# Turning the fourth row group of the first block by a transposing DMA in a fused S5 + SwiGLU kernel

## The chip, the cores and the metric

The kernel runs on one core of a Trainium2 chip. The metric is the device time of one execution in microseconds, lower is better. The core's engines are named as the profile names them: PE (TensorE, matrix products; PEld is its weight load), DVE (VectorE), ACT (ScalarE), POOL (GpSimd) and SP (SyncE, which here only issues DMAs).

## The reference

The input `x` has 2048 rows of 512 values. Its layer norm feeds two branches, and their sum with `x` is the output.

```python
def reference(x, Lambda_re, Lambda_im, B_re, B_im, C_re, C_im, log_dt, Dskip, w1, w3, w2):
    xn = layernorm(x)                                   # over the 512 values of a row
    Lam, dt = Lambda_re + 1j * Lambda_im, exp(log_dt)
    Lam_bar = exp(dt * Lam)
    B_bar = ((Lam_bar - 1) / Lam)[:, None] * (B_re + 1j * B_im)
    Bu = xn @ B_bar.T                                   # 2048 x 512, complex
    h[t] = Lam_bar * h[t - 1] + Bu[t]                   # recurrence over the rows
    ssm = 2 * (h @ (C_re + 1j * C_im).T).real + xn * Dskip
    glu = (silu(xn @ w1) * (xn @ w3)) @ w2              # 512 -> 1792 -> 512
    return x + ssm + glu
```

All tensors are bfloat16.

## The kernel before

The 2048 rows are cut into four blocks of 512 (`TBLK`), and a block into four row groups of 128. For the products over the 512 columns PE needs the normalised rows turned, columns on partitions: `xnT` holds a block as 4 x 128 columns by 512 rows. The 1792 features of `w1` and `w3` are cut into 14 groups of 128; the text calls such a group "a feature" and counts from 0.

The order of work on every engine is the program's order, written by hand (`manual_schedule`). It runs: the first block's layer norm and turning, `glu_up(0)` (products with w1 and w3, Silu and Copy on ACT, their product `hgT` on DVE), `ssm_in(0)` and `ssm_in(1)` (products with B), `glu_up(1)`, `y_out(0)` (products with w2 and C, output), and so on to `y_out(3)`. DVE's work of the recurrence, of the later blocks' layer norms (`ln_tasks`) and of the residual (`res_tasks`) is kept in a queue of tasks; `drain(rate)` in the loops above takes tasks from it by their assumed cost.

In blocks 1 to 3 the normalised rows are turned by transposing DMAs on SP (L232). In the first block PE turns them: `turn(c, ...)` issues four 128x128 transposes of row group `c` into a PSUM bank, `put(c, ...)` copies the result into `xnT`, on ACT for groups 0 and 1, on DVE for groups 2 and 3. Between these, `ahead(w_sbs, features, c, n)` issues the products of features 0 to 2 (`B3`) with row groups `c` to `c+n-1`, so that PE works on the groups that are there. The tiles of these three features, `begun`, hold six of the eight PSUM banks; `xt_a` and `xt_b`, the banks of the turned groups, hold the other two. `pprm`, the turned parameters of the recurrence, lies in `xt_a`; `par_cols` copies it on ACT. `glu_up(0)` then adds row group 3 to the features in `begun` (matmuls 128 wide) and makes the rest 512 wide; each feature's g and u tiles need a free PSUM bank.

SP's loads are issued in program order: two row groups of `x_blk[0]`, columns of features 0 to 3 of w1 and w3 in two parts each, of features 4 to 7, `x_blk[1]`, features 8 to 13, `dskip_row`, the turned B (`bt`, eight transposing DMAs), `x_blk[2]`. The parameters and the other two row groups of `x_blk[0]` come on ACT's queue. `load_rest` (w2, `x_blk[3]`, turned C) is a task of the queue.

Of the kernel before, what the change touches and what calls it, by code (L numbers as in the profile page):

```python
# [16 lines left out]
P = 128  # L17
# [3 lines left out]
def kernel(  # L21
# [24 lines left out]
    nc = tc.nc  # L46
# [8 lines left out]
    NDT = D // P  # L55
    NPT = PS // P
    NFT = F // P
# [3 lines left out]
    xv = A_x[0].rearrange("(b c p) d -> p b c d", p=P, c=CPB)  # L61
# [8 lines left out]
    def ps_tile(name):  # L70
        return psum.tile([P, 512], FP32, name=name, tag="ps")


    x_blk = [xpool.tile([P, CPB, D], BF16, name="x_blk") for _ in range(NBLK)]
# [7 lines left out]
    w1_sb = const.tile([P, NDT, F], BF16, name="w1_sb")  # L82
    w3_sb = const.tile([P, NDT, F], BF16, name="w3_sb")
    w2_sb = const.tile([P, NFT, D], BF16, name="w2_sb")
    w1v = B_w1.rearrange("(t p) f -> p t f", p=P)
    w3v = B_w3.rearrange("(t p) f -> p t f", p=P)

    H = NDT // 2

    def load_w13(f0, f1, parts=1):  # L90
        fs = slice(f0 * P, f1 * P)
        for w_sb, wv in ((w1_sb, w1v), (w3_sb, w3v)):
            for i in range(parts):
                ds = slice(i * NDT // parts, (i + 1) * NDT // parts)
                nc.sync.dma_start(out=w_sb[:, ds, fs], in_=wv[:, ds, fs])

    dskip_row = const.tile([P, D], BF16, name="dskip_row")
    bt = [const.tile([P, NDT, PS], BF16, name=f"bt{ri}") for ri in range(2)]
    ct = [const.tile([P, NPT, D], BF16, name=f"ct{ri}") for ri in range(2)]

    def load_turned(dst, src):
        for t in range(NDT):
            nc.sync.dma_start_transpose(out=dst[:, t, :], in_=src[:, t * P:(t + 1) * P])
# [9 lines left out]
    load_prm(1, A_Lambda_im, nc.scalar)  # L113
    load_prm(2, A_log_dt, nc.scalar)
    load_w13(0, 4, 2)
    load_w13(4, 8)
    nc.sync.dma_start(out=x_blk[1], in_=xv[:, 1, :, :])
    load_w13(8, NFT)
    nc.sync.dma_start(out=dskip_row, in_=A_Dskip.partition_broadcast(P))
    load_turned(bt[0], A_B_re)  # L120
    load_turned(bt[1], A_B_im)
    nc.sync.dma_start(out=x_blk[2], in_=xv[:, 2, :, :])

    def load_rest():
        nc.sync.dma_start(out=w2_sb, in_=B_w2.rearrange("(t p) d -> p t d", p=P))
# [19 lines left out]
    begun = [(ps_tile("g_ps"), ps_tile("u_ps")) for _ in range(3)]  # L145
# [13 lines left out]
    xnTs = [None] * NBLK  # L159
# [28 lines left out]
    def normed(c, parts=1):  # L188
        xn = work.tile([P, D], BF16, name="xn", bufs=8)
        for i in range(parts):  # L190
            ds = slice(i * D // parts, (i + 1) * D // parts)
            nc.vector.tensor_scalar(out=xn[:, ds], in0=x_blk[c // CPB][:, c % CPB, ds], scalar1=mv_all[:, c, 0:1],
                                    scalar2=rstd_all[:, c:c + 1], op0=ALU.subtract, op1=ALU.mult)
        return xn
# [49 lines left out]
    xt_a = psum.tile([P, 2 * NDT, P], BF16, name="xt_ps", tag="ps")  # L244
    xt_b = psum.tile([P, 2 * NDT, P], BF16, name="xt_ps", tag="ps")
    pprm = xt_a[:, NDT]
    xn0 = xns_of[0] = {}

    def turn(c, pxt, d0=0, d1=NDT):
        for dt in range(d0, d1):  # L250
            nc.tensor.transpose(out=pxt[:, dt - d0, :], in_=xn0[c][:, dt * P:(dt + 1) * P], identity=ident)  # L251

    def put(c, pxt, eng, d0=0, d1=NDT):
        dst = xnTs[0][:, d0:d1, c * P:(c + 1) * P]
        if eng is nc.scalar:
            nc.scalar.activation(out=dst, in_=pxt, func=ACT.Copy)
        else:
            nc.vector.tensor_copy(out=dst, in_=pxt)
# [10 lines left out]
    def par_cols():  # L269
        prmc = const.tile([P, 3 * NPT], FP32, name="prmc")  # L270
        nc.scalar.activation(out=prmc, in_=pprm[:, :3 * NPT], func=ACT.Copy)
        col["lre"], col["lim"], col["ldt"] = (prmc[:, i * NPT:(i + 1) * NPT] for i in range(3))
        nc.scalar.activation(out=c4("dt"), in_=col["ldt"], func=ACT.Exp)
        nc.gpsimd.tensor_tensor(out=c4("kr"), in0=col["dt"], in1=col["lre"], op=ALU.mult)
        nc.gpsimd.tensor_tensor(out=c4("ki"), in0=col["dt"], in1=col["lim"], op=ALU.mult)
        nc.gpsimd.tensor_scalar(out=c4("turn"), in0=col["ki"], scalar1=float(1.0 / (2.0 * np.pi)), scalar2=None,
                                op0=ALU.mult)
        tt = nc.gpsimd.tensor_tensor
        tt(out=c4("den"), in0=col["lre"], in1=col["lre"], op=ALU.mult)
        tt(out=c4("d2"), in0=col["lim"], in1=col["lim"], op=ALU.mult)  # L280
        tt(out=col["den"], in0=col["den"], in1=col["d2"], op=ALU.add)
# [87 lines left out]
    def glu_mm(b, f, w_sb, ps, ts, dts=range(NDT), joins=False):  # L369

        for dt in dts:
            nc.tensor.matmul(out=ps[:, ts], lhsT=w_sb[:, dt, f * P:(f + 1) * P], rhs=xnTs[b][:, dt, ts],  # L372
                             start=(dt == 0 and not joins), stop=(dt == NDT - 1))
# [128 lines left out]
    def ahead(w_sbs, fs, c, n=1, dts=range(NDT), joins=False):  # L502
        for f in fs:
            for w_sb in w_sbs:
                glu_mm(0, f, w_sb, begun[f][w_sb is w3_sb], slice(c * P, (c + n) * P), dts, joins)

    t1 = [ps[:, :P].bitcast(BF16).rearrange("p (t c) -> p t c", c=P) for ps in begun[2]]
    ta, tb, t2, t3 = xt_a[:, :H], xt_b[:, :H], xt_b[:, NDT:], xt_a[:, :NDT]

    stats(0)  # L510
    aggr(0)
# [19 lines left out]
    B3 = (0, 1, 2)  # L531
    lo, hi = range(H), range(H, NDT)
# [5 lines left out]
    rstd_act(3, 4)  # L538
    ahead((w3_sb,), B3, 0, 2, lo)
    turn(2, t2)  # L540
    put(2, t2, nc.vector)
    xn0[3] = normed(3)
    ahead((w3_sb,), B3, 0, 2, hi)
    nc.tensor.transpose(out=pprm, in_=prm, identity=ident)  # L544
    par_cols()
    ahead((w1_sb, w3_sb), (0,), 2)
    turn(3, t3)
    put(3, t3, nc.vector)
    nc.scalar.activation(out=r_col, in_=col["kr"], func=ACT.Exp)
    nc.scalar.preload_act_table_set("silu_and_others")  # L550
    ahead((w1_sb, w3_sb), (1, 2), 2)

    push([(3.2, par_turns), (0.2, par_recip)])
    push([(0.0, lambda: for_act.extend(par_trig()))])
# [53 lines left out]
```

## Time and profile before

| what | value |
|---|---|
| median of 3 runs | 211.85 us (211.66 to 211.96) |
| profiled execution | 212.11 us |
| its span, first to last instruction | 210.3 us |
| granted TensorE clock | 1.00 throughout |
| PE busy | 206.6 us (98%) |
| DVE busy | 173.5 us (82%) |
| ACT busy | 93.4 us (44%) |
| DMA bytes | 13.69 MB, mean 65 GB/s |

The share of busy time is an average over the span; the chain that ended last says which engine's work followed on which without a gap. A timeline row gives start, duration, engine, line, operation and tiles. Matmuls overlap in PE's pipeline, so the cost of a matmul is the distance to the next start, not its duration. "SPq" rows are the issue of DMAs; "to landing" is from the start of the issue to the signal that the data are there.

### The profile page before, as it was taken

What the parts mean: (1) busy time and instruction counts of PE and PEld (TensorE: products, weight loads), DVE (VectorE), ACT (ScalarE), POOL (GpSimd) and SP (SyncE); (2) the same over time, 40 slices, a digit from 0 to 9 for tenths busy, and PEclk for the clock granted to TensorE, in tenths of its full rate; (3) what the DMA queues carried; (4) which work ended last, traced back from release to release, by engine and by line L of the source; (5) the groups of instructions that cost most, each with busy time, mean ns of one, the idle gap of its engine ahead of it and who ended that gap; (6) DMA issues with size and microseconds to landing.
All of it is one profiled execution on the core that took longest, in us unless ns stands there. A gap on an engine that the chain in (4) does not pass through costs nothing.

```text
span 210.3 us, 2878 instructions
## 1 busy us (share of the span) xinstructions
PE 206.6 (98%) x1036; PEld 97.7 (46%) x1036; DVE 173.5 (82%) x346; ACT 93.4 (44%) x167; POOL 6.0 (3%) x27
## 2 busy tenths in 40 slices
PE   8999999999999999999999999999999999999994
PEld 3864444444444444444444444444444444444453
DVE  4699989989999999999999999999999999121111
ACT  3599967666666200066666600036666620000000
POOL 2010320000000000000000000000000000000000
PEclk9999999999999999999999999999999999999999
DMA  5999599944000000000004200100000000000110
GB/s 165 294 366 219 109 178 325 217 106 100 0 3 0 0 25 25 28 26 0 0 0 77 28 1 24 50 25 5 0 0 0 0 3 25 27 25 25 34 44 25
DMA packets 25014, 13.69 MB, mean 65 GB/s; under 512 B 15912, under 2 KB 25000, under 8 KB 25000
## 3 DMA queue, kind: packets, MB, share of 16 engines
q1 hardware_dynamic: 24704, 13.24, 26.1%
q10 hardware_dynamic: 296, 0.27, 0.4%
q8 instruction: 8, 0.13, 0.3%
q14 instruction: 6, 0.05, 0.1%
HBM read 7.74 MB, written 2.10 MB: 47 GB/s over the span
## 4 chain that ended last, share of the span: by engine, by line
PE 96%; DMA 2%; SPq 0%; DVE 0%; issue 0%
PE g_ps L372 23%; PE u_ps L372 23%; PE y_ps L488 23%; PE y_ps L493 13%; PE bu_ps L411 13%; DMA w_sb<-in_B_w_dram 2%; SPq L77 0%; PE xt_ps L251 0%; DVE o L498 0%; PE xt_ps L544 0%
## 5 line engine op out<-in xcount | busy, mean ns | idle before, releaser
L372 PEld LDWEIGHTS <-w_sb 128*128 128x128 bf16 x502 | 46.4, 98 | 50.6 <-DMA w_sb<-in_B_w_dram 0.6
L372 PE MATMUL g_ps<-xnT,w_sb 128*128 128x512 bf16 (+2 forms) x254 | 58.2, 354 | 0.3 <-DMA w_sb<-in_B_w_dram 0.3
L372 PE MATMUL u_ps<-xnT,w_sb 128*128 128x512 bf16 (+2 forms) x248 | 58.4, 358 | 0.0
L488 PE MATMUL y_ps<-w_sb,hgT 128*128 128x512 bf16 (+2 forms) x238 | 51.2, 366 | 0.0
L390 ACT ACTIVATE up<-u_ps 128x512 bf16<-128x512 f32 x56 | 34.0, 607 | 14.9 <-PE u_ps L372 14.9
L413 ACT ACTIVATE u<-bu_ps 128x512 bf16<-128x512 f32 x32 | 19.1, 597 | 46.3 <-PE bu_ps L411 46.3
L388 ACT ACTIVATE sl<-g_ps 128x512 bf16<-128x512 f32 x56 | 34.0, 608 | 9.9 <-PE g_ps L372 9.2
L445 DVE TENSOR_TENSOR_SCAN ab<-r_col,h,ab 128x256 bf16<-128x256 f32 x56 | 37.7, 733 | 0.2
L488 PEld LDWEIGHTS <-hgT 128*128 128x128 bf16 x238 | 22.8, 98 | 25.9
L498 DVE TENSOR_TENSOR o<-y_ps,x_blk 128x512 bf16<-128x512 f32 (+2 forms) x17 | 11.1, 654 | 24.3 <-PE y_ps L493 24.3
L493 PE MATMUL y_ps<-ct,h 128*128 128x512 bf16 (+2 forms) x136 | 30.4, 366 | 0.0
L411 PE MATMUL bu_ps<-xnT,bt 128*128 128x512 bf16 x128 | 28.1, 379 | 0.0
L397 DVE TENSOR_TENSOR hgT<-sl,up 128x512 bf16<-128x512 bf16 x56 | 22.9, 414 | 2.1 <-ACT up L390 2.1
L493 PEld LDWEIGHTS <-h 128*128 128x128 bf16 x136 | 13.0, 98 | 14.7
L411 PEld LDWEIGHTS <-bt 128*128 128x128 bf16 x128 | 12.5, 98 | 15.1
L164 DVE BATCH_NORM_STATS2 stats<-x_blk 128x6 f32<-128x512 bf16 x16 | 10.6, 675 | 2.5 <-DMA x_blk<-in_A_x_dram 2.5
L454 DVE TENSOR_TENSOR ab<-ab,tab_s 128x2048 bf16<-128x2048 bf16 x8 | 9.8, 1222 | 0.2
L450 DVE TENSOR_TENSOR ab<-ab,tab_c 128x2048 bf16<-128x2048 bf16 x8 | 9.8, 1222 | 0.1
L427 DVE TENSOR_TENSOR ab<-u,tab_x 128x2048 bf16<-128x2048 bf16 x8 | 9.7, 1219 | 0.0
L430 DVE TENSOR_TENSOR ab<-u,tab_y 128x2048 bf16<-128x2048 bf16 x8 | 9.7, 1218 | 0.0
L201 DVE TENSOR_TENSOR x_blk<-xd,x_blk 128x512 bf16<-128x512 bf16 x16 | 6.8, 426 | 0.5
L200 DVE TENSOR_TENSOR xd<-xn,dskip_row 128x512 bf16<-128x512 bf16 x16 | 6.7, 418 | 0.0
(76 smaller groups left out, 81.3 us busy)
## 6 DMA issues: line engine op xcount, KB each, us to landing
out_dram<-o SPq DMA_DIRECT2D x15, 128.0 KB, 1.7
w_sb<-in_B_w_dram SPq DMA_DIRECT2D x1, 1792.0 KB, 9.3
x_blk<-in_A_x_dram SPq DMA_DIRECT2D x3, 512.0 KB, 6.3
w_sb<-in_B_w_dram SPq DMA_DIRECT2D x2, 768.0 KB, 7.8
w_sb<-in_B_w_dram SPq DMA_DIRECT2D x4, 256.0 KB, 5.0
w_sb<-in_B_w_dram SPq DMA_DIRECT2D x2, 512.0 KB, 4.1
x_blk<-in_A_x_dram SPq DMA_DIRECT2D x2, 128.0 KB, 2.2
x_blk<-in_A_x_dram ACTq DMA_DIRECT2D x1, 256.0 KB, 4.7
```

The lines of the kernel that those rows point to most:

```text
L164: nc.vector.bn_stats(out=sums[c], in_=x_blk[c // CPB][:, c % CPB, :])
L372: nc.tensor.matmul(out=ps[:, ts], lhsT=w_sb[:, dt, f * P:(f + 1) * P], rhs=xnTs[b][:, dt, ts], start=(dt == 0 and not joins), stop=(dt == ...
L388: nc.scalar.activation(out=sl16, in_=g_ps, func=ACT.Silu)
L390: nc.scalar.activation(out=up16, in_=u_ps, func=ACT.Copy)
L397: nc.vector.tensor_tensor(out=hg[b][:, f, :], in0=sl16, in1=up16, op=ALU.mult)
L411: nc.tensor.matmul(out=u_ps, lhsT=bt[ri][:, dt, pt * P:(pt + 1) * P], rhs=xnTs[b][:, dt, :], start=(dt == 0), stop=(dt == NDT - 1))
L413: nc.scalar.activation(out=u16[:, :, pt, ri, :], in_=u_ps.rearrange("p (s t) -> p s t", s=NSB), func=ACT.Copy)
L445: nc.vector.tensor_tensor_scan(out=a[:, pt, 2 * ri + 1, :], data0=r_b, data1=a[:, pt, 2 * ri, :], initial=init, op0=ALU.mult, op1=ALU.add)
L450: nc.vector.tensor_tensor(out=a[:, :, 0::2, :], in0=a[:, :, 1::2, :], in1=tab_b("c"), op=ALU.mult)
L488: nc.tensor.matmul(out=y_ps[:, ds], lhsT=hg[b][:, f, cl * P:(cl + 1) * P], rhs=w2_sb[:, f, ds], start=(f == 0), stop=False)
L493: nc.tensor.matmul(out=y_ps[:, ds], lhsT=h_tiles[i][:, pt, ri, h_ts], rhs=ct[ri][:, pt, ds], start=False, stop=(pt == NPT - 1 and ri == 1))
L498: nc.vector.tensor_tensor(out=o16[:, ds], in0=y_ps[:, ds], in1=x_blk[b][:, cl, ds], op=ALU.add)
```

## The change

- The fourth row group (c = 3) of the first block is turned by one transposing DMA on SP, from its normalised rows straight into `xnT`. The four transposes on PE and the copy on DVE go; the tile view `t3` goes.
- The SP loads from w3 of features 4 to 7 on are put into a function `load_next`, called right behind that DMA. The w1 load of features 4 to 7 stays ahead of it.
- On DVE the normalising of group 3 now comes before `put` of group 2.
- On PE the transpose of `prm`, and with it `par_cols`, moves ahead of the second half of w3's products with groups 0 and 1.
- A fourth pair of PSUM tiles is added to `begun`: the products of feature 3 are issued with the others, first w1 on groups 0 and 1, then group 2 of features 0 to 2, then w3 on groups 0 and 1 and both weights on group 2. `glu_up(0)` finishes four features with row group 3, not three.

```diff
     load_w13(0, 4, 2)
-    load_w13(4, 8)
-    nc.sync.dma_start(out=x_blk[1], in_=xv[:, 1, :, :])
-    load_w13(8, NFT)
-    nc.sync.dma_start(out=dskip_row, in_=A_Dskip.partition_broadcast(P))
-    load_turned(bt[0], A_B_re)
-    load_turned(bt[1], A_B_im)
-    nc.sync.dma_start(out=x_blk[2], in_=xv[:, 2, :, :])
+    nc.sync.dma_start(out=w1_sb[:, :, 4 * P:8 * P], in_=w1v[:, :, 4 * P:8 * P])
+
+    def load_next():
+        nc.sync.dma_start(out=w3_sb[:, :, 4 * P:8 * P], in_=w3v[:, :, 4 * P:8 * P])
+        nc.sync.dma_start(out=x_blk[1], in_=xv[:, 1, :, :])
+        load_w13(8, NFT)
+        nc.sync.dma_start(out=dskip_row, in_=A_Dskip.partition_broadcast(P))
+        load_turned(bt[0], A_B_re)
+        load_turned(bt[1], A_B_im)
+        nc.sync.dma_start(out=x_blk[2], in_=xv[:, 2, :, :])
...
-    ta, tb, t2, t3 = xt_a[:, :H], xt_b[:, :H], xt_b[:, NDT:], xt_a[:, :NDT]
+    ta, tb, t2 = xt_a[:, :H], xt_b[:, :H], xt_b[:, NDT:]
...
     ahead((w3_sb,), B3, 0, 2, lo)
     turn(2, t2)
+    xn0[3] = normed(3)
     put(2, t2, nc.vector)
-    xn0[3] = normed(3)
-    ahead((w3_sb,), B3, 0, 2, hi)
+    nc.sync.dma_start_transpose(out=xnTs[0][:, :, 3 * P:], in_=xn0[3])
+    load_next()
     nc.tensor.transpose(out=pprm, in_=prm, identity=ident)
     par_cols()
-    ahead((w1_sb, w3_sb), (0,), 2)
-    turn(3, t3)
-    put(3, t3, nc.vector)
+    ahead((w3_sb,), B3, 0, 2, hi)
+    begun.append((ps_tile("g_ps"), ps_tile("u_ps")))
+    ahead((w1_sb,), (3,), 0, 2)
+    ahead((w1_sb, w3_sb), B3, 2)
+    ahead((w3_sb,), (3,), 0, 2)
+    ahead((w1_sb, w3_sb), (3,), 2)
     nc.scalar.activation(out=r_col, in_=col["kr"], func=ACT.Exp)
     nc.scalar.preload_act_table_set("silu_and_others")
-    ahead((w1_sb, w3_sb), (1, 2), 2)
```

## The prediction

> **What bounds the kernel now.** I read the page's busy rows and its chain that ended last, PE's waits, then the timeline of the first 30 us, then single DMA issues with their times to landing.
>
> ```profile
> span 210.3 us, 2878 instructions
> PE 206.6 (98%) x1036; PEld 97.7 (46%) x1036; DVE 173.5 (82%) x346; ACT 93.4 (44%) x167; POOL 6.0 (3%) x27
> ...
> PE 96%; DMA 2%; SPq 0%; DVE 0%; issue 0%
> ```
> ```profile
> PE g_ps L150 <- PEq L592: 0.8, 1, 0.8
> PE g_ps L372 <- DMA w_sb<-in_B_w_dram: 0.3, 1, 0.3
> ```
>
> PE is busy 98% of the span and holds 96% of the chain. The second fence is all that PE waited for: 0.8 us at the start, and 0.3 for the first weights, which end at 6.48 us (the chain's 2% DMA). From there to the end PE never waits. So the time moves by exactly two things: PE work added or removed, and PE waits added. The timeline around the change (start, duration, engine):
>
> ```profile
> 8.46 0.20 ACT L172 ACTIVATE rstd_all<-rstd_all 128x1 f32<-128x1 f32 x1
> 8.49 0.39 PE L251 MATMUL xt_ps<-ident,xn 128*128 128x128 bf16 x4
> ...
> 8.72 0.82 PE L372 MATMUL u_ps<-xnT,w_sb 128*128 128x256 bf16 x6
> 8.92 0.42 DVE L258 COPY xnT<-xt_ps 128x512 bf16<-128x512 bf16 x1 [0.73 <-PE xt_ps L251]
> 9.26 0.40 DVE L192 TENSOR_SCALAR xn<-x_blk,mv_all,rstd_all 128x512 bf16<-128x512 bf16 x1
> ...
> 9.37 0.22 PE L544 MATMUL xt_ps<-ident,prm 128*128 128x128 bf16 x1
> ...
> 9.88 0.39 PE L251 MATMUL xt_ps<-ident,xn 128*128 128x128 bf16 x4
> ...
> 10.10 0.39 PE L372 MATMUL g_ps<-xnT,w_sb 128*128 128x128 bf16 x4
> ...
> 12.33 1.03 PE L372 MATMUL g_ps<-xnT,w_sb 128*128 128x512 bf16 x4
> ...
> 13.20 1.03 PE L372 MATMUL u_ps<-xnT,w_sb 128*128 128x512 bf16 x4
> ```
>
> Durations overlap in PE's pipeline, so costs are differences of starts: four transposes 9.88 to 10.10, 0.22; four 128-wide matmuls 0.2225 (10.10 to 10.99 is four such sets); six 256-wide 8.72 to 9.37, 0.65, so 0.433 for four; four 512-wide 12.33 to 13.20, 0.864; the turn of `prm` 0.06.
>
> Two DMA prices follow, from the rows of single issues: the transposing DMA at 111.17 (ring empty) and the 512 KB load of `w1_sb` columns 4 to 8 (issued 6.45).
>
> ```profile
> L232 SPq DMA_TRANSPOSE xnT<-xn x1: 1201/1201/1201, 111.2 to 111.2; - x1
> ...
> DMA to landing us min/median/max: 2.3/2.3/2.3
> ```
> ```profile
> w_sb<-in_B_w_dram SPq DMA_DIRECT2D x1, 512.0 KB, 4.1
> ```
>
> A transposition holds SP 1.2 us and lands 2.3 us after its issue began.
>
> **Part 1, PE work.** Removed: four transposes, 0.22. Feature 3 (index from 0) of columns 0 to 511 is done as 256+128+128 in place of 512: per weight 0.433+0.2225+0.2225 = 0.878 for 0.864, twice, +0.03. Laid out from the last unchanged start, 8.72: `prm` to 8.78, the w3 half of features 0 to 2 to 9.43, feature 3 w1 to 9.86, six sets of group 2 (1.335) to 11.20, feature 3 w3 to 11.63, its two sets of group 2 to 12.08. There `glu_up` needs group 3 for the first time (10.99 before). Eight sets of group 3 end at 13.86, where feature 4 starts; before it was 14.06. So **-0.20** if PE never waits. DVE's `put` of group 3 (0.42) goes too, off the path.
>
> **Part 2, the new wait for the transposition.** DVE has group 3's rstd at 8.66 and normalises at once, 8.72 to 9.13, since `put` of group 2 now stands behind it. SP starts 0.16 after such an end (the row at 110.60 lasts 0.41, SP starts at 111.17), so at 9.29, and the data land at 9.29+2.3 = 11.6. PE wants them at 12.08: hidden by 0.5, cost 0 taken. The cover is the fourth feature and group 2, 2.65 us of matmuls from 9.43. Ends: 2.3 (ring empty) and 4.7 (the transposition at 24.94, directly behind a 512 KB load), which would land at 13.99 and cost 1.9. I take the near end, because the load ahead on this ring was issued 2.84 us before, not 0.7, and should land near 6.45+4.1 = 10.55.
>
> The VectorE page of the Trainium skill ("VectorE: DVE Perf Modes", section The three transpose paths) speaks against the change: it gives a 128x128 block 390 ns on TensorE and 1309 ns on the DMA crossbar, and advises TensorE. By its figure four blocks in a row would be 5.24 us (an estimate), landing at 14.53, and the sum 2.45-0.20, some 2.2 us slower; the rows here, 2.3 to 4.7 for the same four blocks, replace it.
>
> **Part 3, PSUM.** The fourth pair of tiles needs both banks of `xt_a` and `xt_b`. One is free after the copy of `pprm` on ACT (about 9.2), the other after DVE's `put` of group 2, now 9.17 to 9.59. If the w1 tile takes the second, PE waits from 9.43 to 9.65: 0 to 0.22. The trace doesn't show which; I take 0, and part 4 would swallow most of it.
>
> **Part 4, the loads moved behind it on SP.** Behind the waiting SP stand, in order, w3 columns 4 to 8, `x_blk[1]`, w1 and w3 from 8, `dskip_row`, eight turned loads of B, `x_blk[2]`. The first was issued at 6.86 and is now at 9.29+1.22+0.04 = 10.55. PE wants it for feature 4's up half at 13.86+0.86 = 14.72. With 4.1 it lands at 14.65, just in time. But a load that follows transpositions moves data later: `x_blk[2]`, issued 24.23 right behind such DMAs, against w1's of 6.45 (window, us, clock, DMA share, GB/s):
>
> ```profile
> 7.20:7.40 0.20, 1.00 0.16 46
> 7.40:7.60 0.20, 1.00 0.89 97
> ...
> 25.20:25.60 0.40, 1.00 0.06 18
> 25.60:26.00 0.40, 1.00 0.34 108
> ```
>
> Data start 0.95 after the issue there, 1.4 here, so 4.5 in place of 4.1 (an estimate): landing 15.05, a wait of **+0.33**, the value taken. Ends: 4.1 (no wait) and 6.3, the row of `x_blk[1]`, 512 KB among other loads (landing 16.85, a wait of 2.13).
>
> The others are covered. `x_blk[1]` lands about 1.4 behind, 16.4 (13.7 before); DVE's statistics, at 14.64 now, stall some 1.8, and `hgT` of feature 2 behind them goes to about 17.0, while ACT wants its `sl16` buffer for feature 6 at 19.27; DVE waits 1.26 at 47.75, so its lag ends there. Were that cover gone, PE would wait out the rest, at most 1.8. w1 from 8 landed at 15.8, is some 2.8 later, 18.6, and is wanted at 20.8. The last turned load of B goes from 22.9 to about 26, lands 2.7 later at 28.7, wanted at 32.3. The transpositions of block 1 land about 34, wanted at 38.4. ACT's first Silu moves from 11.88 to 12.5; feature 4's PSUM bank is then free at 13.1, wanted at 13.86. Cost 0.
>
> **Sum.** -0.20+0.33 = +0.13 against the profiled execution's 212.11 (span 210.3), which lies 0.26 above the median 211.85. So 211.98, put as 212.0. About 0.2% (0.42 us) is what this measurement can tell from no change.
>
> **Rivals.** (a) *The transposition queues.* The load of w1 columns 4 to 8 is still in flight at 9.29. If the transposition meets it as at 24.94 and 26.3 (4.7 and 4.1), it lands at 13.4 to 14.0, PE waits 1.3 to 1.9, and the time is 213.0 to 213.6. It decides from 3.4 us to landing (12.7). For it: those two rows. Against it: 2.84 us of head start. The DMA page of the Trainium skill ("DMA: Bandwidth & Descriptors", section Queues, rings and completion order) says that an engine consumes a ring's descriptors in order; the rows at 24.94 agree. Chance 0.14.
>
> (b) *The w3 load lands late*, at 5.0 to 6.3 after issue, as the first 256 KB loads (4.8 to 5.2) and `x_blk[1]` (6.3) did in company. PE waits 0.83 to 2.13 at feature 4: +0.63 to +1.93, 212.5 to 213.8. It is slower by over 0.42 from 4.8 on. For it: it is the first load issued again after 2.6 us, with 2 MB issued right behind it. Against it: so was w1's at 6.45, with 4.1. Chance 0.20.
>
> (c) *Faster.* With no wait at all 211.65, which is inside the 0.2%. For more, a wait of before would have to go: past the start PE's only one is the 0.3 for the first weights, whose issues stand unchanged ahead of the edit. Without it the time would be 211.35. Chance 0.06.
>
> **Numbers.** Forecast 0.60 (211.6 to 212.3: the w3 load landing 4.1 to 4.8 after its issue), (a) 0.14, (b) 0.20, (c) 0.06. Faster 0.06, same 0.60, slower 0.34. The range 211.5 to 213.2 takes in the forecast, the lower part of (a) and most of (b).
>
> **What would show it.** After: twelve transposes on PE, not sixteen; one more transposing DMA near 9.3 landing near 11.6; group 3's first matmul at 12.1 without idle time before it; feature 4's up half at 15.05 with some 0.3 idle, released by the w3 load; its gate half at 13.86. Idle time before group 3 means (a), over 0.8 before feature 4's up half means (b), 0.2 before feature 3 means the PSUM bank. Wrong in kind would be a wait after 25 us, say for B or for `x_blk[2]`, which I price at nothing.

## The result, and the profile after

The changed kernel takes 212.41 us (median of 10 runs, 212.05 to 212.60) against 211.81 (211.62 to 211.96) for the kernel before: a ratio of 1.0028, 95% interval 1.0018 to 1.0037. It is slower by 0.6 us. The profiled execution took 212.46 us, 0.35 more than that of before. From the page of the profile after:

```profile
PE 206.3 (98%) x1048; PEld 97.9 (46%) x1048; DVE 173.3 (82%) x345; ACT 93.2 (44%) x167; POOL 6.6 (3%) x27
...
PE 91%; DMA 4%; DVE 1%; ACT 1%; SPq 0%; issue 0%
```

PE's share of the chain fell from 96 to 91%; DMA's rose from 2 to 4%, and DVE and ACT have 1% each. PE's waits (us in total, times, longest) name two more than before, the second and the fourth:

```profile
PE g_ps L153 <- PEq L598: 0.8, 1, 0.8
PE u_ps L375 <- DMA w_sb<-in_B_w_dram: 0.4, 1, 0.4
PE g_ps L375 <- DMA w_sb<-in_B_w_dram: 0.3, 1, 0.3
PE xt_ps L254 <- DVE xn L195: 0.2, 1, 0.2
```

The fourth is at 4.91, ahead of the first weights, for which PE waits anyway. The timeline shows where the second is:

```profile
8.60 0.41 DVE L195 TENSOR_SCALAR xn<-x_blk,mv_all,rstd_all 128x512 bf16<-128x512 bf16 x1 [0.51 <-ACT rstd_all L175]
...
9.03 1.30 SPq L546 DMA_TRANSPOSE xnT<-xn  x1
...
10.39 0.57 SPq L119 DMA_DIRECT2D w_sb<-in_B_w_dram  x1
...
11.76 0.39 PE L375 MATMUL u_ps<-xnT,w_sb 128*128 128x128 bf16 x4
11.98 0.39 PE L375 MATMUL g_ps<-xnT,w_sb 128*128 128x128 bf16 x4
...
13.77 1.03 PE L375 MATMUL g_ps<-xnT,w_sb 128*128 128x512 bf16 x4
...
15.17 1.04 PE L375 MATMUL u_ps<-xnT,w_sb 128*128 128x512 bf16 x4 [0.38 <-DMA w_sb<-in_B_w_dram]
...
16.60 0.69 DVE L167 BATCH_NORM_STATS2 stats<-x_blk 128x6 f32<-128x512 bf16 x1 [1.58 <-DMA x_blk<-in_A_x_dram]
```

SP starts the transposition 0.02 us after DVE's normalised rows. PE passes to row group 3 at 11.98 without a gap, 0.22 after the set before it. Feature 4's up half comes 1.40 us after its gate half, 0.864 without a wait, so 0.54 is lost to the w3 load issued at 10.39. (The 0.38 in brackets is less, since ends of matmuls are modelled.) The chain that ended last shows what that load hangs on:

```profile
1.53 4.62 DMA x_blk<-in_A_x_dram
...
8.60 0.41 DVE xn L195
9.01 0.34 DVE xnT L261
9.35 0.99 SPq L546
...
10.39 4.74 DMA w_sb<-in_B_w_dram
...
15.17 1.04 PE u_ps L375 x4
```

(It puts SP's release down to DVE's copy that ends at 9.34, though the issue had begun at 9.03, when the rows of L195 were there.) Before, the chain ran through the first weights and then PE alone. Now it runs from the last rows of `x_blk[0]` through the layer norm on DVE and ACT to SP, the load, and PE.

### The profile page after: what moved, and what is told of

The parts are those of the page before. It is cut to its first block, busy times and chain, and to the rows that moved or that the text cites. A ratio compares the mean times of both kernels' runs of the same rounds, so it can differ in the third digit from the quotient of the medians.

```text
span 210.7 us, 2902 instructions
## 1 busy us (share of the span) xinstructions
PE 206.3 (98%) x1048; PEld 97.9 (46%) x1048; DVE 173.3 (82%) x345; ACT 93.2 (44%) x167; POOL 6.6 (3%) x27
## 4 chain that ended last, share of the span: by engine, by line
PE 91%; DMA 4%; DVE 1%; ACT 1%; SPq 0%; issue 0%
PE y_ps L491 23%; PE u_ps L375 21%; PE g_ps L375 21%; PE y_ps L496 13%; PE bu_ps L414 13%; DMA w_sb<-in_B_w_dram 2%; DMA x_blk<-in_A_x_dram 2%; SPq L546 0%; DVE xn L195 0%; ACT L81 0%; DVE stats L167 0%; ACT rstd_all L175 0%; ACT rstd_all L174 0%; DVE xnT L261 0%; DVE mv_all L170 0%
## 5 line engine op out<-in xcount | busy, mean ns | idle before, releaser
L375 PEld LDWEIGHTS <-w_sb 128*128 128x128 bf16 x518 | 47.1, 98 | 50.4 <-DMA w_sb<-in_B_w_dram 1.4
L195 DVE TENSOR_SCALAR xn<-x_blk,mv_all,rstd_all 128x512 bf16<-128x512 bf16 (+1 forms) x18 | 6.3, 392 | 0.6 <-ACT rstd_all L175 0.5
```

## The experiments

Two theories at first. L (the late load): PE's work is 0.2 us less, the wait for w3 of features 4 to 7 eats that and more, and nothing else happened. R (a rest elsewhere): part of the 0.60 us has another source, because the pair of profiles shows 0.35 only. Diffs are against the changed kernel unless said.

**same_again.** No edit.

> The changed kernel itself, unaltered, on the same chip as the next ones. Both theories: about 212.4 us (before 211.8), with feature 4's up half starting 1.4 us after its gate half instead of 0.86, because the w3 load of features 4 to 7 lands at about 15.1. Theory L (the late load): the wait of about 0.54 us, less 0.2 us of PE work saved, is all there is, and the median lies 0.35 to 0.6 above before according to when that load lands in a run. Theory R (a rest elsewhere): the profile explains only 0.35 of the 0.60 us between the medians, and 0.25 us come from something that the trace of PE doesn't show.

Measured: 212.18 us against 211.79, ratio 1.0017 (1.0007 to 1.0027). In its profile SP issued the transposition at 8.85, and the up half followed 0.96 us after the gate half:

```profile
13.76 1.03 PE L375 MATMUL g_ps<-xnT,w_sb 128*128 128x512 bf16 x3
14.72 1.04 PE L375 MATMUL u_ps<-xnT,w_sb 128*128 128x512 bf16 x4
```

The wait is 0.10 here, 0.54 in the first profile: its size differs between executions, and the total with it (212.00 and 212.46). The w3 load was issued 0.19 earlier here (10.20, not 10.39), as the last rows of `x_blk[0]` came earlier, and it took 4.47 us to land, not 4.74; PE's own marks up to there are the same to 0.01.

**halves_4_6.**

```diff
-    nc.sync.dma_start(out=w1_sb[:, :, 4 * P:8 * P], in_=w1v[:, :, 4 * P:8 * P])
+    load_w13(4, 6)
     def load_next():
-        nc.sync.dma_start(out=w3_sb[:, :, 4 * P:8 * P], in_=w3v[:, :, 4 * P:8 * P])
+        load_w13(6, 8)
```

> The same bytes ahead of the transposing DMA as in the change, but w1 and w3 of features 4 and 5 (256 KB each) instead of w1 of features 4 to 7 (512 KB); behind it both weights of features 6 and 7. PE wants the loads behind the transposition at 17.2 us instead of 14.6, and they should land by about 15.5. Theory L: no wait of PE past 6.5 us but the first weights' own, and the time is 0.2 below before: 211.6 us. Theory R: the wait goes, 0.54 us, but the rest stays: 211.85 us, the same as before.

Measured: 211.88 against 211.79, ratio 1.0011 (0.9997 to 1.0026). Three of its twelve runs lie at 212.44 to 213.11, the other nine at 211.67 to 212.08.

```profile
13.50 1.03 PE L375 MATMUL g_ps<-xnT,w_sb 128*128 128x512 bf16 x3
14.36 1.03 PE L375 MATMUL u_ps<-xnT,w_sb 128*128 128x512 bf16 x4
```

The wait is gone in this trace, yet the median is R's (211.85), not L's (211.6): a rest exists, though not on PE, which in this trace is 0.18 us ahead of before from w3's first products (7.46) on.

**w3_ahead.**

```diff
-    nc.sync.dma_start(out=w1_sb[:, :, 4 * P:8 * P], in_=w1v[:, :, 4 * P:8 * P])
+    load_w13(4, 8)
     def load_next():
-        nc.sync.dma_start(out=w3_sb[:, :, 4 * P:8 * P], in_=w3v[:, :, 4 * P:8 * P])
```

> The w3 load of features 4 to 7 is issued ahead of the transposing DMA again, so that 1 MB stands in front of it on SP's ring and not 512 KB. Theory Q (the transposition has to queue behind the loads of its ring): the load's data end at about 11.2 us and the transposition lands some 1.9 us later, near 13.0; PE, which wants row group 3 at 12.0, waits about 1 us, and no longer for w3: 212.6 us. Rival (a transposition takes 2.3 us whatever is on the ring): it lands at 11.4, nothing waits, 211.6 us.

Measured: 212.05 against 211.79, ratio 1.0019 (1.0000 to 1.0039). SP issued the transposition at 8.82; PE got to row group 3 at 12.20, 0.21 late:

```profile
11.76 0.39 PE L374 MATMUL u_ps<-xnT,w_sb 128*128 128x128 bf16 x4
12.20 0.38 PE L374 MATMUL g_ps<-xnT,w_sb 128*128 128x128 bf16 x4
```

With 1 MB ahead on the ring it is slower, 3.3 us from issue to landing and 3.4 to PE's start, but by less than I expected (4.0, from 9.03 to 13.0). Its first packets move 1.9 us after its issue, at 10.73, when the last of the loads ahead go; in the profile after they move 1.3 us after the issue, at 10.32, when the 512 KB ahead have been gone since 9.8. The DMA page of the Trainium skill ("DMA: Bandwidth & Descriptors", section Queues, rings and completion order) has descriptors of a ring consumed in order on each engine; the order of the packets in this trace agrees.

**three_features.**

```diff
-    begun.append((ps_tile("g_ps"), ps_tile("u_ps")))
-    ahead((w1_sb,), (3,), 0, 2)
     ahead((w1_sb, w3_sb), B3, 2)
-    ahead((w3_sb,), (3,), 0, 2)
-    ahead((w1_sb, w3_sb), (3,), 2)
```

> The change without the fourth feature: group 3 is still turned by DMA and the loads are still behind it, but PE has only group 2 of three features to do in the meantime (1.3 us from 9.3 on). This shows when the transposition lands, which the change hides. Theory: it lands 2.3 to 2.4 us after its issue at 9.03, so at 11.4; PE wants it at 10.65, waits 0.75 us, and reaches feature 4's up half at about 15.2, when w3 is there. The time is about 0.35 to 0.45 above before, 212.2 us. Rival (the transposition is slowed by the w1 load in flight, 3 us or more): a wait of 1.4 us or more and 212.8 us or more.

Measured: 212.41 against 211.79, ratio 1.0025 (1.0014 to 1.0036).

```profile
10.15 0.39 PE L375 MATMUL u_ps<-xnT,w_sb 128*128 128x128 bf16 x4
11.02 0.38 PE L375 MATMUL g_ps<-xnT,w_sb 128*128 128x128 bf16 x4 [0.48 <-DMA xnT<-xn]
```

Issued at 8.51, used at 11.02: 2.5 us with 512 KB ahead, where 2.3 was predicted for the change. PE loses 0.65 (0.87 less 0.222) rather than 0.75, as PE gets there later after the issue than I had reckoned; the median is 0.2 above what was expected. So the fourth feature does what it is there for: it hides this wait, which the change without it pays.

**early_turn.**

```diff
-    nc.sync.dma_start_transpose(out=xnTs[0][:, :, 3 * P:], in_=xn0[3])
+    nc.sync.dma_start_transpose(out=xnTs[0][:, :, 3 * P:], in_=xn0[1])
```

> The changed kernel with one operand altered: the transposing DMA reads the normalised rows of group 1, ready at 5.3 us, not those of group 3 (so the products of row group 3 are computed from group 1's rows). SP then doesn't wait for DVE, the loads behind go out some 2 us earlier, and neither the transposition nor the w3 load can be late. What is left is the change in PE's work alone. Theory L: 0.2 us below before, 211.6 us, and from the start of w3's first products to the last matmul 199.0 us in the trace (199.22 before, 199.59 after). Theory R: something else in the change costs 0.2 to 0.25 us, and the time is that of before, 211.8, or above.

Measured: 211.65 against 211.77, ratio 0.9994 (0.9985 to 1.0002). From 7.76 to the last group of matmuls at 206.79 it is 199.03 us, as theory L had it, and no wait is left behind the first weights. The medians lie 0.12 us apart, less than the 0.2, and the interval takes in no difference at all; -0.18 of PE work and +0.09 at the end (both read below) would make -0.09. PE's work and the number of DMAs are those of the change, and only the time at which the transposition and the loads behind it go out differs. So the late issue is what costs the change its 0.60 and 0.39: against their own runs of before it lies 0.72 and 0.51 above early_turn.

**x_before_w3.**

```diff
-        nc.sync.dma_start(out=w3_sb[:, :, 4 * P:8 * P], in_=w3v[:, :, 4 * P:8 * P])
         nc.sync.dma_start(out=x_blk[1], in_=xv[:, 1, :, :])
+        nc.sync.dma_start(out=w3_sb[:, :, 4 * P:8 * P], in_=w3v[:, :, 4 * P:8 * P])
```

> The changed kernel with the first two loads behind the transposition swapped: 512 KB of x_blk[1] go ahead of w3 of features 4 to 7. The suspected wait is made longer by a known amount: w3 is issued 0.6 us later and lands behind 512 KB at 370 GB/s, 1.4 us later, at about 16.5. Theory L (PE waits for this load and nothing hides it): the wait grows by 1.4 to 2 us and so does the time, to 213.6 to 214.3. Rival (the load's wait is mostly hidden by other slack): less than half of that, under 213.1.

Measured: 213.41 against 211.77, ratio 1.0078 (1.0065 to 1.0091).

```profile
13.28 1.03 PE L375 MATMUL g_ps<-xnT,w_sb 128*128 128x512 bf16 x4
16.00 1.04 PE L375 MATMUL u_ps<-xnT,w_sb 128*128 128x512 bf16 x4 [1.69 <-DMA w_sb<-in_B_w_dram]
```

The wait is 2.72-0.864 = 1.86 us, and the total is 1.64 above before: 1.86-0.18 = 1.68. The wait goes into the time whole, to some 0.1 us, with no slack to hide it. From the transposition's issue (8.36) to the up half it is 7.64 us, against 6.14 and 5.87 in the two profiles of the change: 1.5 to 1.8 more, as expected. The median is 0.2 below L's range all the same: it lies 1.0 and 1.2 above the two medians of the change, to which the growth was added, while the profiled waits grew by 1.3 and 1.8. Waits in the unprofiled runs of the change that are longer than the profiled ones would explain that, and early_turn's medians point the same way.

**act_ring.** The transposing DMA on ACT's queue, the loads up to `dskip_row` where they were before.

```diff
-    nc.sync.dma_start_transpose(out=xnTs[0][:, :, 3 * P:], in_=xn0[3])
-    load_next()
     nc.tensor.transpose(out=pprm, in_=prm, identity=ident)
     par_cols()
+    nc.scalar.dma_start_transpose(out=xnTs[0][:, :, 3 * P:], in_=xn0[3])
+    load_next()                    # only bt and x_blk[2]
```

> The loads are issued on SP as in the kernel before, none waits for DVE, and the transposing DMA is issued on ACT's queue, behind the copy and the exponential of par_cols (about 9.1 us). Only x_blk[2] and the turned B stay behind it. It tells whether the transposition is late because of its place in SP's ring or because all transfers share the engines. Theory S (shared engines, in w3_ahead it took 3.4 us from issue to PE's start with 1 MB ahead on its own ring): 3 us or more here too, landing at 12.1 or later, PE waits 0.2 to 1 us before row group 3, 211.8 to 212.6 us. Rival (a ring of its own brings it past the loads): it lands within 2.5 us, nothing waits, and the time is 211.6.

Measured: 220.12 against 211.77, ratio 1.0401 (1.0378 to 1.0424). The issue at 9.01 took 9.5 us to land; the first fence is PE's wait, the second the windows (us, granted clock, DMA share, GB/s):

```profile
PE g_ps L374 <- DMA xnT<-xn: 6.6, 1, 6.6
```
```profile
15.00:16.00 1.00, 1.00 0.06 9
16.00:17.00 1.00, 0.74 1.08 338
17.00:18.00 1.00, 0.50 1.10 382
```

A ring of its own does not bring it past the 3 MB of loads issued on SP by then: its own packets move from 13.3 to 17.7, side by side with those of the last loads, with next to nothing moving from 15 to 16 us, and it lands at 18.5. The direction was S's, the size far off. With the loads held back, on SP's ring, it took 2.5 us; the run changes the ring and the loads at once, so how much of the 7 us is due to each is not shown, nor why the traffic stopped for a microsecond. PE's idle time also halved the granted clock from 17 to 23 us: the eight sets of row group 3 took 3.37 us, not 1.78, and feature 4's gate half 1.54, not 0.86, another 2.3. With the 6.7 of the wait (11.63 to 18.58, less 0.22) that is the 9.0 by which the profiled execution (220.76) lies above before. The page "TensorE: Matmul & The Clock Gate" of the Trainium skill (Part 1, on the clock gate) has the clock fall to half after an idle window of some 3.4 us; here it is 0.74 in the stretch that begins 4 us after PE's last matmul (12.0).

**before_again.** The kernel before, no edit.

> The kernel before once more, for a second profile: the first one has its first matmul on real data at 6.48 us and its total 0.3 us above the median of the unprofiled runs. If the arrival of the first weights varies between executions, the first matmul is at another time here and the total moves with it, while the time from the first products of w3 to the last matmul stays 199.2 us.

Measured: 211.66 us.

Every mark from w3's first products on (7.40, 13.62, 14.48) is 0.43 or 0.44 earlier than in the first profile of before, and the total is 0.45 less. The first products with loaded weights start at 5.92, not 6.48: PE does not wait for the weights here, while it waited 0.31 us there. Two profiles of one kernel differ by more than the change's profiled loss. The rows of `x_blk[0]` come earlier too: the statistics of group 2 start at 5.66, not 6.27. Side by side (us; "end" is from the start of the last DVE instruction to the execution's end; DMAs are all issues on SP and ACT):

| run | w3's first products | feature 4, gate | feature 4, up | end | total | DMAs |
|---|---|---|---|---|---|---|
| before | 7.83 | 14.06 | 14.92 | 4.41 | 212.11 | 64 |
| before_again | 7.40 | 13.62 | 14.48 | 4.40 | 211.66 | 64 |
| after | 7.72 | 13.77 | 15.17 | 4.50 | 212.46 | 65 |
| same_again | 7.72 | 13.76 | 14.72 | 4.49 | 212.00 | 65 |
| early_turn | 7.76 | 13.80 | 14.66 | 4.49 | 211.93 | 65 |
| halves_4_6 | 7.46 | 13.50 | 14.36 | 4.64 | 211.78 | 67 |

The distance from w3's first products to feature 4 is 6.22 or 6.23 before, 6.04 or 6.05 in every form of the change without an earlier wait: 0.18 saved. The last columns hold a part of the rest: the end is 0.09 longer in the change, 0.24 in halves_4_6. In halves_4_6 that is nearly all: -0.18+0.24 = 0.06, for 0.09 between the medians.

**w2_in_four** and **sevens** followed. The first is the kernel before with

```diff
-        nc.sync.dma_start(out=w2_sb, in_=B_w2.rearrange("(t p) d -> p t d", p=P))
+        w2v = B_w2.rearrange("(t p) d -> p t d", p=P)
+        for t0, t1 in ((0, 4), (4, 8), (8, 11), (11, NFT)):
+            nc.sync.dma_start(out=w2_sb[:, t0:t1, :], in_=w2v[:, t0:t1, :])
```

> The kernel before with the load of w2, wanted 35 us after it lands, cut into four DMAs: three more on SP, and nothing else. From the last DVE instruction's start to the end of the execution the traces have 4.40 and 4.41 us in the kernel before, 4.49 to 4.50 in six kernels with one DMA more, 4.64 in halves_4_6 with three more. Theory E (each DMA more lengthens the end by 0.08 us): 4.64 here, and 212.0 us in all. Rival (the end has to do with the transposition, or with the loads that it delays): 4.40, and 211.8.

Measured: 212.06 against 211.66, ratio 1.0016 (1.0007 to 1.0025). The end is 212.12-207.48 = 4.64, as theory E had it, and from w3's first products (7.62) to the last group of matmuls (206.83) it is 199.21 us, as before (199.22). Loads that nobody waits for, and no transposition, lengthen the end by 0.24. The median grew by 0.40, so 0.16 of it are not explained.

**sevens.**

```diff
-    nc.sync.dma_start(out=w1_sb[:, :, 4 * P:8 * P], in_=w1v[:, :, 4 * P:8 * P])
+    load_w13(4, 7)
     def load_next():
-        nc.sync.dma_start(out=w3_sb[:, :, 4 * P:8 * P], in_=w3v[:, :, 4 * P:8 * P])
+        nc.sync.dma_start(out=w1_sb[:, :, 7 * P:], in_=w1v[:, :, 7 * P:])
         nc.sync.dma_start(out=x_blk[1], in_=xv[:, 1, :, :])
-        load_w13(8, NFT)
+        nc.sync.dma_start(out=w3_sb[:, :, 7 * P:], in_=w3v[:, :, 7 * P:])
```

> The changed kernel with the loads cut at feature 7: w1 and w3 of features 4 to 6 (384 KB each) ahead of the transposing DMA, then w1 of 7 to 13, x_blk[1], w3 of 7 to 13; as many DMAs as in the change. 768 KB ahead, between 512 KB (2.5 us from issue to PE's start in three_features) and 1 MB (3.4 us in w3_ahead): about 2.9 us, so at 11.5 to 11.9, when PE comes to row group 3. PE wants w1 and w3 of feature 7 at 18.7 and 19.5, and they should land by 15 and by 18.7. Theory L: no wait, or up to 0.2 us before row group 3: PE 0.18 earlier, the end 0.09 later, 211.7 us, below before by no more than can be measured. Rival (the loads behind are late again, or x_blk[1] holds DVE up long enough to stop ACT): a wait of PE and 212.2 us or more.

Measured: 211.89 against 211.66, ratio 1.0006 (0.9997 to 1.0015). No wait at row group 3: the transposition landed 2.51 us after its issue. But there is one at feature 7, 1.17-0.864 = 0.31 us, since w3 of features 7 to 13 landed at 19.74 and not by 18.7. That is the rival's wait, at less than the rival's price (212.2):

```profile
18.62 1.03 PE L375 MATMUL g_ps<-xnT,w_sb 128*128 128x512 bf16 x4
19.79 0.39 PE L375 MATMUL u_ps<-xnT,w_sb 128*128 128x512 bf16 x1
```

**outs_merged.** The kernel before with, in `y_out`,

```diff
+                if b < NBLK - 1:
+                    nc.vector.tensor_tensor(out=x_blk[b][:, cl, :], in0=y_ps, in1=x_blk[b][:, cl, :], op=ALU.add)
+                    if cl == CPB - 1:
+                        nc.sync.dma_start(out=ov[:, b * CPB:(b + 1) * CPB, :], in_=x_blk[b])
+                    continue
                 o16 = work.tile([P, D], BF16, name="o16", bufs=3)
```

> The kernel before with fewer DMAs: the outputs of blocks 0 to 2 are written in place over x_blk and stored as one DMA per block (512 KB) in place of four of 128 KB; nine DMAs fewer on SP, nothing else. Theory E (0.08 us at the end for each DMA): the end from the last DVE instruction's start goes from 4.40 to 3.7 us, and the time to 211.0. Rival (only DMAs near the end of the program, or only more of them, move it): 4.40 and 211.7.

Measured: 212.20 against 211.64, ratio 1.0032 (1.0019 to 1.0045): slower, against both. The end is 212.20-207.22 = 4.98, with nine DMAs fewer. PE is not the cause: from 7.36 to 206.57 it is again 199.21 us. So theory E falls: the number of DMAs alone does not set the end.

SP's last instructions in the traces say more. The DMAs report to eight semaphores (102 to 109) in turn. The last store lands 1.76 to 1.79 us after the start of the last DVE instruction in all these runs, and SP closes the program with five waits in a fixed order that go through the semaphores. What counts is how many waits stand behind the one that the last store releases, up to the drain (SP's next instruction). This was read from the traces afterwards; no run was made to test it:

| DMAs | semaphore of the last store | in SP's wait | waits behind it | from its landing to SP's first drain | end |
|---|---|---|---|---|---|
| 64 (before) | 109 | 5th | 0 | 0.08 | 4.41 |
| 65 (after) | 102 | 3rd | 2 | 0.19 | 4.50 |
| 67 (halves_4_6) | 104 | 1st | 4 | 0.32 | 4.64 |
| 55 (outs_merged) | 108 | 4th | 1 | 0.56 | 4.98 |

A wait behind it takes 0.05 to 0.06 us, so two or four of them are the 0.09 and the 0.24. With 55 only one stands behind, which alone would put the end between those of 64 and 65; there SP lets 0.47 us pass between its last wait and its first drain, while no DMA lands, and 0.13 more than elsewhere behind that drain. That is not explained.

**sevens_outs_merged.** Both edits, and w3 ahead of `x_blk[1]`; 56 DMAs.

> The same merging of outputs, on the changed kernel with the loads cut at feature 7, now with w3 of 7 to 13 ahead of x_blk[1], so that it lands before PE wants it at 19.5. Theories L and E together: PE's work 0.18 us less than in outs_merged, one DMA more (0.08), no wait: 0.1 us below outs_merged, 210.9 us. Rival (x_blk[1], now last, holds DVE up some 4 us, ACT's buffers run full and PE's banks with them): a wait of PE near 20 us, and 0.3 us or more above outs_merged.

Measured: 211.53 against 211.64, ratio 0.9998 (0.9988 to 1.0008). The end is 212.41-208.03 = 4.38: the last store reports to 109 again, and no wait stands behind it. DVE stood 4.4 us for `x_blk[1]` and PE did not feel it. The profile caught one of the two runs above 212.3 of twelve, the other ten being 211.38 to 211.62:

```profile
11.25 0.39 PE L375 MATMUL u_ps<-xnT,w_sb 128*128 128x128 bf16 x4
12.61 0.38 PE L375 MATMUL g_ps<-xnT,w_sb 128*128 128x128 bf16 x4 [0.98 <-DMA xnT<-xn]
```

Issued at 8.35, the transposition landed after 4.22 us and was awaited until 12.61, with the same 768 KB ahead as in sevens, where it landed after 2.51 and PE waited for nothing. Its landing scatters. In the trace 479 of its 512 packets have started by 10.5, while in sevens all have by 10.64, 1.9 us after the issue; the last sixteenth starts from 11.57 to 11.99, behind the last packets of the loads ahead, which start until 11.52. Why these were late is open. By the traces this version saves PE's 0.18 where nothing is late and pays over 0.8 where the transposition is; by its median it cannot be told from the kernel before, and none of the versions beats it.

## Why the prediction was right or wrong

**Part 1** held: -0.20 predicted, -0.18 measured, in every variant.

**Part 2** held: no gap before row group 3. The price of the transposition was 2.5 us to PE's start with 512 KB ahead, not 2.3, and SP's start 0.02 after DVE, not 0.16. The slack of 0.5 us is real but thin. Rival (a) did not come in the change: in the profile after the load ahead had gone (9.8) before the transposition's first packet (10.3); a landing after 3.3 us or more did come with 1 MB ahead (3.33) and once with 768 KB (4.22).

By the 1309 ns for a block of the Trainium skill ("VectorE: DVE Perf Modes", section The three transpose paths) four blocks in a row would take 5.2 us (an estimate); 2.5 for four blocks in one DMA was measured.

**Part 3** held: no gap at feature 3.

**Part 4** had the mechanism, the place and nearly the duration: 4.74 from issue to landing for 4.5, landing at 15.13 for 15.05. The wait was 0.54, not 0.33: PE wanted the load 0.09 earlier (14.63, not 14.72), it landed 0.08 later, and PE started 0.04 after the landing. DVE's stall of 1.58 (1.8 predicted) and all the other moved loads cost nothing, as priced.

**The sum** is the step that came out short: +0.13 was forecast, +0.35 came in the profiles and +0.60 in the medians. From before's profile to the one after it is -0.18 of PE work, +0.54 of wait, +0.09 at the end and -0.11 because w3's first products started earlier (7.72, not 7.83): +0.34. So the wait was mis-sized, by 0.21, and the end of the program, 0.09 longer with a 65th DMA, was not in the sum at all. The start was not in it either. It differs from execution to execution whatever the kernel (w3's first products at 7.22 to 7.83 in the fourteen profiles), and two profiles cannot be compared to 0.4 us without taking it out.

Without the start the change costs +0.45 by the profile after and +0.01 by same_again (-0.18+0.10+0.09), while the medians say +0.60 and +0.39. Waits of some 0.7 and 0.5 in the unprofiled runs would close the gap. Those runs have no trace, but early_turn, which removes the late issue alone, takes 0.72 and 0.51 away. So the cost of the late issue is shown, and the two profiles caught less of it (0.54 and 0.10) than the usual run has; that all of it is the wait for w3 is not shown. An early start does not make the wait longer by itself. In before_again the first weights came early and the rows of `x_blk[0]`, on which the moved load hangs, even more so: from the statistics of group 2 to w3's first products it is 1.56 us in before and 1.74 in before_again, 1.55 in the profile after and 1.73 in same_again. That, and the load's own 4.74 or 4.47, is what the wait scatters with.

So the likeliest case, within 0.2%, did not come: the result is just beyond it, with the sign and the mechanism of the forecast. Rival (b) names the same load, but its condition, a landing 5.0 us or more after the issue, was not met in the two profiles of the change (4.74 and 4.47). The range held the result, in part by luck: the term at the end (0.09) and what the wait had more than forecast (0.21 in the profile) are together larger than the sum. Theory R was right that there was a rest beside the profiled wait; 0.09 of it is the end of the program, and most of the remainder goes when the loads are no longer late.

Still open are the 0.47 us of SP at the end with 55 DMAs, on one profile, and what makes the last packets of a load, and with them the transposition, late in some executions.

## What to carry to other kernels

When a load is moved behind a DMA that waits for computed data, its arrival changes clock: here it followed the rows of `x_blk[0]` and DVE, while its consumer followed the weights and PE. Price it with the scatter of both, not from one profiled execution: the same kernel waited 0.54 us in one and 0.10 in another. Cut what stands ahead of the waiting DMA by when its consumer needs it, so that no load behind it is needed first; and on a kernel that is bound by one engine, a saving of 0.2 us is worth little when it makes the engine depend on landings that scatter by more, as both did here.

## What the runs showed of the hardware

A transposing DMA of 128 KB from SBUF to SBUF landed 2.3 us after its issue on an empty ring, 2.4 with 512 KB of loads ahead (halves_4_6), 2.5 and once 4.2 with 768 KB, 3.3 with 1 MB, and 9.5 on the other ring beside 3 MB of loads. The end of the execution took 4.38 to 4.41, 4.49 or 4.50, and 4.64 us according to where in SP's closing waits the semaphore of the last store stood, and 4.98 in one kernel for a reason that is open. And the first products with loaded weights of one and the same kernel started 0.56 us apart in two executions (5.92 and 6.48), w3's first products 0.43.
